# Three buffers for the first product's weights, and `w_out`'s groups loaded one by one

## The chip, the cores and the metric

The kernel runs on one core of a Trainium2 chip. The metric is the device time of one execution in microseconds (us); each kernel is told by the median of several runs.

## The reference, cut to what matters

```python
# attention: B, H, S, D = 4, 8, 768, 64
q_bits = (q @ proj > 0)                       # 6 bits per row, as one bucket number
k_bits = (k @ proj > 0)
scores = D**-0.5 * q @ k.T                    # where the buckets differ: -1e9
attn   = softmax(scores) @ v
# bridge: (B, H, S, D) -> x of 3072 x 512
h   = x @ w_in                                # 512 x 2048
g   = maximum(h, 0) + alpha * minimum(h, 0)
out = g @ w_out                               # 2048 x 512
```

All inputs and the output are float32 to the kernel's eye; the two weights arrive as pairs of words, which the kernel rounds and joins.

## The kernel before, in words

**Attention.** The function `fast_path` works on 16 pairs of heads (4 batches of 4), each in two units of 384 queries: 32 units of about 10 us. In a unit PE computes scores for 6 blocks of keys (L734), ACT takes their exponential into one of ten `pt` tiles (L739), and PE multiplies these by `v` (`attend`, L767). The sum over the keys is made of two halves: DVE adds blocks 0 and 1 into `accp` and GpSimd's queue (POOL) issues a transfer that adds block 2 to it on the way (`add_first`, L748 and L749); DVE adds blocks 3 to 5 into `accd` (L753, L754) and then `accp` to it (`add_total`, L757). PE sums `accd` over the partitions (`totals`, L779), DVE and GpSimd turn this into a divisor, and the result `x` is stored to device memory (`x_s`, L809).

**Weights.** Beside attention the 32 pieces of the two weights are loaded (`raw`, L567), rounded on ACT and DVE, and stored again. `w_in` goes, with the sums that the fast product below needs, to `w_in_s` (L648): 8 groups of 7 matrices. `w_out` goes as it is to `w_out_r` (L635), in 8 groups; its sums are made later.

**The MLP.** Both products use seven multiplications of half-size blocks in place of eight (the class `Product`). Per batch of 768 tokens there are 8 blocks of the first product, named f_0 to f_7, and 7 of the second, named z_1 z_2 z_5 z_6 z_3 z_7 z_4 in their order. A block's steps are groups of matmuls into PSUM banks `a`, `b`, `c`; ACT copies some of them out, DVE adds others and applies the activation (L896, L900, L904). PE is written to begin the next block (`now.step(1)`) before it makes the last step of the one before (`before.step(4)`), so that f_2a's first group stands ahead of f_1a's last.

- `load_w(n)`, L829, loads a block's seven matrices of `w_in_s` into a `wi` tile (896 KB, tag `wi`, two buffers). `load_w(0)` and `load_w(1)` are called in attention, at unit 18; block n's own pass calls `load_w` for n + 2, whose buffer is free when block n's last step is done.
- `load_out(n)`, L934, loads two groups of `w_out_r` into one `wo` tile (2 transfers of 512 KB on GpSimd's queue). The tile shares its tag `wl` and two buffers with the second product's weights.
- `sum_out(n)`, L942, makes a group's four sums on DVE (L946) and stores the group to `w_out_s` (L947, GpSimd's queue). The sums are spread by hand over the first seven blocks of batch 0 (0; 1; 2; 3 and 4; 5; 6 and 7, in blocks 1 to 6). Every second call loads two more groups.
- `load_w2(b, n)`, L923, loads the second product's weights (1 MB) into a `wl` tile, from `w_out_r` or `w_out_s`, on SP's queue; DVE makes further sums of it (`ws`, L964) and of `g` (`gs`, L972). In batch 0 the first two of these loads take over the buffers of the last `wo` tiles, and so wait for the stores of groups 4 to 7.
- In block 4 of batch 0 four small transposes on PE and some tiny DVE instructions check the inputs' magnitude (`verdict`); for inputs out of range a general path would run after it.

**What sets the order.** Instructions of PE, DVE, ACT and most of GpSimd are kept in the order of the program (`do` is `tc.keep_in_program_order`). Transfers on SP's queue and GpSimd's are not: the framework places each by its own planning, and gives it the waits that its buffers and data need. Tiles live in pools; the pool `sb` of attention is closed when attention ends, and the pool `late` opens over its memory. The pool `mid` (with `wi`) and `const` last for the whole program.

The line numbers here and below are those of the kernel before.

Of the kernel before, what the change touches and what calls it, by code (L numbers as in the profile page):

```python
# [8 lines left out]
F32 = mybir.dt.float32  # L9
BF16 = mybir.dt.bfloat16  # L10
# [396 lines left out]
def fast_path(  # L407
# [12 lines left out]
    nc = tc.nc  # L420
    P = 128
    B, H, S, D = q.shape
    NB = proj.shape[1]
    NTOK, DM = out.shape
# [20 lines left out]
    const = ctx.enter_context(tc.tile_pool(name="const", bufs=1))  # L445
    dram = ctx.enter_context(tc.tile_pool(name="dram", bufs=1, space=bass.MemoryType.DRAM))
    mid = ctx.enter_context(tc.tile_pool(name="mid", bufs=2))
    psum = ctx.enter_context(tc.tile_pool(name="ps", bufs=1, space=bass.MemoryType.PSUM))
    attn = ctx.enter_context(ExitStack())
    pool = attn.enter_context(tc.tile_pool(name="sb", bufs=2))  # L450
# [13 lines left out]
    alpha = const.tile([P, NF], F32, name="alpha")  # L464
    mags = const.tile([P, 2, NPAIR], F32, name="mags")

    qbs = [const.tile([P, S], BF16, name=f"qb{i}") for i in range(2)]
    NI = NF // 2
    NM = 7
    w_in_s = dram.tile([NI, P, NM, 2, P], F32, name="w_in_s")  # L470
    w_out_r = dram.tile([4, P, NI, DM // 2], F32, name="w_out_r")
# [31 lines left out]

    def setup():

        zero = const.tile([P, 512], BF16, name="zero")
        do(DVE.memset(zero, 0.0))
        do(DVE.memset(wh, 0.0))
        for s in range(2):
            nc.sync.dma_start(wh[D * s : D * s + D, :NB], proj)  # L510
        nc.sync.dma_start(alpha16, moe_alpha.rearrange("(t p) -> t p", p=P))
        make_identity(nc, ident)
        do(DVE.memset(ones, 1.0))

        ps = psum.tile([P, 512], F32, name="nil", tag="av")
        nil.append(lambda: do(PE.matmul(ps, zero[:, :P], zero, start=True, stop=True)))
        for i in range(7):
            nil[0]()

        do(DVE.memset(hb, 0.0))  # L520
        for r in range(0, P, 32):
            do(DVE.memset(hb[r : r + 2 * NB], 1.0 if r % D else -1.0))
            do(DVE.memset(hb[r : r + NB], -1e-37))

        do(DVE.tensor_scalar(hb_k[:, 0:1], hb, -1.0, None, op0=ALU.mult))
        do(DVE.memset(hb_k[:, 1:2], 0.0))
        for r in range(0, P, 32):
            do(DVE.memset(hb_k[r : r + 2 * NB, 1:2], 0.5))
        for t in pts:
            do(POOL.memset(t[:, :, CW : CW + 1], 1.0))  # L530
        for t in qbs:
            do(POOL.memset(t, 0.0))
# [9 lines left out]
    HW = NW // 2  # L542
# [39 lines left out]
    def weight_clamp(i):  # L582
        if i < NW:
            i = order[i]
            x = wx[i]
            do(DVE.tensor_scalar(x, x, HI_MIN, None, op0=ALU.max, op1=ALU.max, accum_out=wmax[:, i : i + 1]))
# [225 lines left out]
    x_m, w_m, g_m = {}, {}, {}  # L812

    def load_x(b):
        for m, kh, ch in ((0, 0, 0), (1, 1, 0), (2, 1, 1), (5, 0, 1)):
            t = mid.tile([P, 2, CW], F32, name=f"x{b}_{m}", tag=f"x{m}", bufs=1)
            nc.sync.dma_start(
                t, x_s[b, 2 * kh : 2 * kh + 2].rearrange("k p s -> p k s")[:, :, ch * CW : (ch + 1) * CW],
            )
            x_m[b, m] = t  # L820
# [8 lines left out]
    def load_w(n):  # L829

        if n < B * NI:
            w_m[n] = mid.tile([P, NM, 2, P], F32, name=f"wi{n}", tag="wi")
            nc.sync.dma_start(w_m[n], w_in_s[n % NI])

    class Product:
# [96 lines left out]
    w_o = {}  # L932

    def load_out(n):  # L934

        if n < NI:
            t = late[0].tile([P, 2, 4, DM // 2], F32, name=f"wo{n}", tag="wl")
            for i in range(2):
                nc.gpsimd.dma_start(t[:, i], w_out_r[:, :, n + i].rearrange("m p d -> p m d"))
                w_o[n + i] = t[:, i]  # L940

    def sum_out(n):  # L942

        w = w_o[n]
        for to, x, op, y in ((2, 3, ALU.add, 2), (3, 0, ALU.subtract, 3), (0, 2, ALU.subtract, 0), (1, 1, ALU.subtract, 0)):
            do(DVE.tensor_tensor(w[:, to], w[:, x], w[:, y], op=op))  # L946
        nc.gpsimd.dma_start(w_out_s[:, :, n].rearrange("m p d -> p m d"), w)  # L947
        if n % 2:
            load_out(n + 3)

    def sides_g(b, n):
        t = g_m[b, SIDES[ORDER[n]][1]]
# [100 lines left out]
    def verdict():  # L1053
        ps = psum.tile([1, 4, P], F32, name="vd", tag="sm")
        for n in range(4):
            do(PE.transpose(ps[:, n], top[:, n : n + 1], ident))
        do(DVE.tensor_reduce(row, ps, axis=mybir.AxisListType.X, op=ALU.max))
        do(DVE.tensor_tensor(row[:, 0:1], row[:, 0:1], row[:, 1:2], op=ALU.mult))

        do(DVE.tensor_scalar(row[:, 0:1], row[:, 0:1], SAFE, None, op0=ALU.is_le))  # L1060
        do(DVE.tensor_scalar(row[:, 2:3], row[:, 2:3], HI_END, None, op0=ALU.is_lt))
        do(DVE.tensor_scalar(row[:, 3:4], row[:, 3:4], 1.0, None, op0=ALU.is_le))
        do(DVE.tensor_tensor(row[:, 0:1], row[:, 0:1], row[:, 2:3], op=ALU.mult))
        do(DVE.tensor_tensor(row[:, 0:1], row[:, 0:1], row[:, 3:4], op=ALU.mult))
        do(DVE.tensor_scalar(flag, row[:, 0:1], -1.0, 1.0, op0=ALU.mult, op1=ALU.add))
# [37 lines left out]
    for u in range(UNITS):  # L1103
        pi, g = divmod(u, NCH)

        def weight_rest():
            weight_sum(u)
            weight_group(u)
            weight_clamp(u + 1)

        scores(u, 1)
        if u < last:
            scores(u + 1, 0)
        if u:
            divide(u - 1, weight_rest)
        else:
            weight_clamp(1)
        load_weight(u + 3)
        add_last(u)
        add_total(u)  # L1120
        if u < last:
            add_first(u + 1)
        else:
            now = ff1(0, 0)
            now.step(1)
            now.step(5)
        if g == 0 and pi + 1 < NPAIR:
            hash_bits(pi + 1)
        if g == 1 and pi + 2 < NPAIR:
            turn(pi + 2, "q")  # L1130
            turn(pi + 2, "k")
        if u < last:
            weight_parts(u + 1)
        weight_sums(1)
        attend(u)
        totals(u)
        if u == last:
            divide(u)
        if g == 1 and pi + 2 < NPAIR:
            load(pi + 2, "v")  # L1140
        if u == HW + 2:
            load_w(0)
            load_w(1)
            load_x(0)
        if HW + 4 <= u < HW + 8:
            sum_x(0, u - HW - 4, DVE)
        if u + 2 < NW:
            weight_abs(u + 2)
        if u == 1:
            setup_alpha()  # L1150
        if g == 1:
            for name in "qk":
                magnitude(pi, name)
                if pi + 3 < NPAIR:
                    load(pi + 3, name)


    late = []
    attn.close()
    late.append(ctx.enter_context(tc.tile_pool(name="late", bufs=2)))  # L1160
    load_out(0)
    load_out(2)
    blocks = [(b, what, n) for b in range(B) for what, count in (("1", NI), ("2", 7)) for n in range(count)]


    for j, (b, what, n) in enumerate(blocks):
        n2 = n + 1 if what == "2" else 0 if n == NI - 1 else 7
        if n2 == 0:
            sides_g(b, 0)
            sum_w2(b, 0, 3, 4)  # L1170
        now.step(2) if j else now.step(6)
        if j == 0:
            now.step(3)
            now.step(7)
            now.step(2)
        now.step(22)
        if j == 4:
            largest()
        if 0 < n2 < 7:
            sides_g(b, n2)  # L1180
            sum_w2(b, n2, 3, 4)
        if n2 < 7:
            sum_g2(b, n2, 3, 4)
        if j:
            now.step(5)
            now.step(6)
            now.step(3)
            sum_w2(b, n2, 6)
            now.step(7)
            sum_w2(b, n2, 5)  # L1190
            sum_g2(b, n2, 5)
        if j == 4:
            verdict()
        for n_out in [(), (0,), (1,), (2,), (3, 4), (5,), (6, 7)][j] if j < 7 else ():
            sum_out(n_out)
        if what == "1":
            load_w(b * NI + n + 2)

            if 0 <= n - NI + (4 if b else 2) < 2:
                load_w2(b, n - NI + (4 if b else 2))  # L1200
        else:
            load_w2(b, n + 2)
            if b + 1 < B:
                if n == 0:
                    load_x(b + 1)
                if n == 6:
                    for m in range(4):
                        sum_x(b + 1, m, DVE)
        if j + 1 < len(blocks):
            turn_out()  # L1210
        else:
            turn_last(0)
        before = now
        if j + 1 < len(blocks):
            b1, what1, n1 = blocks[j + 1]
            now = ff1(b1, n1) if what1 == "1" else ff2(b1, n1)
            now.step(1)
        before.step(4)
        if n2 < 7:
            sum_g2(b, n2, 6)  # L1220
# [29 lines left out]
```

## Time and profile before

| | |
|---|---|
| median of 7 runs | 905.38 us (903.31 to 906.36) |
| the profiled execution: its own time, its span | 903.01 us, 901.2 us |
| busy: PE, PEld, DVE, ACT, POOL | 887.6, 591.0, 754.8, 408.8, 100.4 us |
| granted PE clock | 1.00 |
| moved by DMA | 146.88 MB, mean 163 GB/s |
| `wi` loads | 32 of 896 KB, 4.6 us to landing (median) |
| `wo` loads and stores | 8 and 8 of 512 KB, 5.8 and 4.8 us (median) |
| `accp` transfers | 32 of 384 KB, 5.2 us (median) |

PE is TensorE's matmuls, PEld its weight loads, DVE is VectorE, ACT ScalarE, POOL GpSimd, SP SyncE, whose queue (SPq) issues most transfers. In a timeline a row has its start and length in us from the span's start, the engine, the line, the operation with out<-in and shapes, the number of instructions merged, and in brackets the idle time before it with what ended it. The lines themselves stand in the prediction. Attention lasts until about 350 us in this execution; the four batches of the MLP follow, 136 us each.

### The profile page before, as it was taken

The numbers are of one execution on the slowest core, as the hardware profiler recorded it, in microseconds if no ns is written. First come the engines' busy times: TensorE is split into PE (matmuls) and PEld (weight loads), VectorE is DVE, ScalarE is ACT, GpSimd is POOL, SyncE is SP. The second block draws the span as 40 slices with busy tenths as digits, with TensorE's granted clock in tenths as the row PEclk, the third lists the DMA queues.
The fourth block names the chain that finished last, engine by engine and source line by source line (L and its number), as shares of the span: only waits on it lengthen the run. The fifth ranks groups of instructions, "written<-read, shape, count | busy, mean of one in ns | idle before, by whom it ended". The sixth has DMA issues, their size and how long they took to land.

```text
span 901.2 us, 15654 instructions
## 1 busy us (share of the span) xinstructions
PE 887.6 (98%) x5885; PEld 591.0 (66%) x5885; DVE 754.8 (84%) x1353; ACT 408.8 (45%) x733; POOL 100.4 (11%) x194
## 2 busy tenths in 40 slices
PE   8999999999999999999999999999999999999996
PEld 4444445444444445556997557998557998556996
DVE  4888988988998996799989668988768989768985
ACT  6888888887888863222112222112222111222111
POOL 1222222222222232120000000000000000000000
PEclk9999999999999999999999999999999999999999
DMA  8778889698798665478343525243525242521242
GB/s 222 177 200 181 204 224 219 167 268 236 166 245 204 179 160 189 155 239 301 135 154 86 183 85 190 94 158 82 187 83 192 95 158 75 194 83 41 95 147 67
DMA packets 131909, 146.88 MB, mean 163 GB/s; under 512 B 78304, under 2 KB 118000, under 8 KB 128240
## 3 DMA queue, kind: packets, MB, share of 16 engines
q1 hardware_dynamic: 118800, 124.03, 44.4%
q0 software_dynamic: 11008, 20.97, 11.8%
q8 instruction: 48, 0.79, 0.4%
q10 hardware_dynamic: 2016, 0.79, 0.3%
q14 instruction: 37, 0.30, 0.1%
HBM read 104.87 MB, written 28.31 MB: 148 GB/s over the span
## 4 chain that ended last, share of the span: by engine, by line
PE 93%; DMA 3%; DVE 1%; SPq 0%; issue 0%; ACT 0%; ACTq 0%
PE sc L734 17%; PE av L767 14%; PE z_2a L854 2%; PE f_0a L854 2%; PE f_2a L854 2%; PE f_5a L854 2%; PE z_4a L854 2%; PE z_7a L854 2%; PE z_3a L854 2%; PE z_6a L854 2%; PE z_5a L854 2%; PE f_3a L854 2%; PE f_6a L854 2%; PE f_4a L854 2%; PE f_1a L854 2%; PE z_1a L854 2%
## 5 line engine op out<-in xcount | busy, mean ns | idle before, releaser
L739 ACT ACTIVATE pt<-sc 128x768 f32<-128x768 f32 x192 | 152.8, 813 | 46.6 <-PE sc L734 44.3
L734 PE MATMUL sc<-qT,kT 64*128 64x384 f32 x768 | 155.3, 482 | 0.0
L767 PE MATMUL av<-pt,vn 128*32 128x384 f32 (+1 forms) x1536 | 130.6, 488 | 0.0
L767 PEld LDWEIGHTS av<-pt,vn 128*32 128x32 f32 x1536 | 46.6, 109 | 75.1 <-issue 72.9
L734 PEld LDWEIGHTS sc<-qT,kT 64*128 64x128 f32 x768 | 68.2, 188 | 35.1 <-issue 34.9
L904 DVE TENSOR_TENSOR g<-g,g 128x384 f32<-128x384 f32 x128 | 68.4, 555 | 2.2
L734 PE MATMUL sc<-qb,kb 64*128 64x384 bf16 x384 | 63.4, 324 | 2.1 <-ACT kb L722 1.0
L749 POOL DMA_DIRECT2D accp<-pt x32 | 38.6, 1205 | 191.2 <-issue 86.5
L972 DVE TENSOR_TENSOR gs<-g,gs 128x768 f32<-128x768 f32 x56 | 53.3, 952 | 1.0
L964 DVE TENSOR_TENSOR ws<-wl 128x512 f32<-128x512 f32 x56 | 38.5, 687 | 17.8 <-DMA wl<-w_out_s 15.9
L972 DVE TENSOR_TENSOR gs<-g 128x768 f32<-128x768 f32 x56 | 53.3, 951 | 0.0
L900 DVE SCALAR_TENSOR_TENSOR g<-h,alpha 128x384 f32<-128x384 f32 x32 | 19.7, 617 | 26.8 <-ACT h L893 26.8
L734 PEld LDWEIGHTS <-kb 64*128 64x128 bf16 x384 | 19.3, 94 | 33.4 <-issue 11.3
L711 ACT ACTIVATE qb<-hs,hb 32x384 bf16<-32x384 f32 x62 | 35.5, 572 | 1.1
L757 DVE TENSOR_TENSOR accd<-accd,accp 128x768 f32<-128x768 f32 x32 | 30.7, 958 | 4.4 <-DMA accp<-pt 3.4
L754 DVE TENSOR_TENSOR accd<-accd,pt 128x768 f32<-128x768 f32 x32 | 30.7, 958 | 3.3
L748 DVE TENSOR_TENSOR accp<-pt,pt 128x768 f32<-128x768 f32 x32 | 30.5, 952 | 2.7 <-ACT pt L739 2.7
L753 DVE TENSOR_TENSOR accd<-pt,pt 128x768 f32<-128x768 f32 x32 | 30.4, 949 | 0.0
L803 POOL COPY rr<-rr 32x6 f32<-32x6 f32 x64 | 27.6, 431 | 2.6
L984 DVE TENSOR_TENSOR m<-m,m 128x768 f32<-128x768 f32 (+1 forms) x36 | 27.1, 751 | 0.7
L722 ACT ACTIVATE kb<-hs,hb 64x384 bf16<-64x384 f32 (+1 forms) x47 | 27.1, 577 | 0.6
L802 POOL COPY rr<-rr 32x6 f32<-32x6 f32 x64 | 19.8, 310 | 65.5 <-DVE rr L799 64.2
(336 smaller groups left out, 1807.2 us busy)
## 6 DMA issues: line engine op xcount, KB each, us to landing
wi<-w_in_s SPq DMA_DIRECT2D x32, 896.0 KB, 4.6
wl<-w_out_s SPq DMA_DIRECT2D x16, 1024.0 KB, 4.8
accp<-pt POOLq DMA_DIRECT2D x32, 384.0 KB, 5.2
wl<-w_out_r SPq DMA_DIRECT2D x12, 1024.0 KB, 4.8
raw<-in_moe_w_out_dram SPq DMA_DIRECT2D x16, 512.0 KB, 5.3
raw<-in_moe_w_in_dram SPq DMA_DIRECT2D x16, 512.0 KB, 4.6
w_in_s<-wsi SPq DMA_DIRECT2D x16, 448.0 KB, 5.8
vn<-in_v_dram SPq DMA_DIRECT2D x16, 384.0 KB, 6.1
```

The costliest lines, as they stand in the source:

```text
L711: do(ACT.activation(bits["q", pi][D * s : D * s + 32, cols], ps["q"][c : c + 32, half, :CW], AF.Sign, bias=hb[c : c + 32],))
L734: do(PE.matmul(sc[:, s, :CW], what["k", pi][r, ks], what["q", pi][r, qs], start=first, stop=not first,))
L739: do(ACT.activation(pt[:, :, :CW], sc[:, :, :CW], AF.Exp, scale=SCALE / DOWN))
L748: do(DVE.tensor_tensor(accp[u], p(u, 0), p(u, 1), op=ALU.add))
L749: nc.gpsimd.dma_start(accp[u], p(u, 2), accum_op=ALU.add)
L754: do(DVE.tensor_tensor(accd[u], accd[u], p(u, 5), op=ALU.add))
L757: do(DVE.tensor_tensor(accd[u], accd[u], accp[u], op=ALU.add))
L767: do(PE.matmul(av[u][D * s + t : D * s + t + 32, :w], nat["v", pi][:, s, kc * D + t : kc * D + t + 32], prob[u, kc][:, s, :w], start=(kc = ...
L854: do(PE.matmul(self.ps[bank], self.left(left, k), self.right(right, k), start=start and k == 0, stop=k == self.nk - 1, skip_group_check=no ...
L904: do(DVE.tensor_tensor(new_g(b, to)[:, i], g_m[b, x][:, i], g_m[b, y][:, i], op=ALU.subtract))
L964: do(DVE.tensor_tensor(t, w2[b, n, x], w2[b, n, y], op=op))
L972: do(DVE.tensor_tensor(t, g2[b, n, x], g2[b, n, y], op=ALU.subtract))
```

## The change

The first product's weights get three buffers. Their third load is called in attention, at unit 25, and every block then calls the load for three blocks ahead. To make room, the tiles `qb` and `zero`, which only attention uses, go from the lasting pool to attention's own. `load_out` loads one group instead of two; group 0 is loaded as before ahead of the blocks, and the others are called in blocks 0 to 4 (1; 2; 3; 4 and 5; 6 and 7), instead of groups 1 to 3 with it and the rest behind sums 1 and 3.

```diff
-    qbs = [const.tile([P, S], BF16, name=f"qb{i}") for i in range(2)]
+    qbs = [pool.tile([P, S], BF16, name=f"qb{i}", bufs=1) for i in range(2)]
...
-        zero = const.tile([P, 512], BF16, name="zero")
+        zero = pool.tile([P, 512], BF16, name="zero", bufs=1)
...
-            w_m[n] = mid.tile([P, NM, 2, P], F32, name=f"wi{n}", tag="wi")
+            w_m[n] = mid.tile([P, NM, 2, P], F32, name=f"wi{n}", tag="wi", bufs=3)
             nc.sync.dma_start(w_m[n], w_in_s[n % NI])
...
     def load_out(n):
 
-        if n < NI:
-            t = late[0].tile([P, 2, 4, DM // 2], F32, name=f"wo{n}", tag="wl")
-            for i in range(2):
-                nc.gpsimd.dma_start(t[:, i], w_out_r[:, :, n + i].rearrange("m p d -> p m d"))
-                w_o[n + i] = t[:, i]
+        if n % 2 == 0:
+            w_o[n] = late[0].tile([P, 2, 4, DM // 2], F32, name=f"wo{n}", tag="wl")
+        nc.gpsimd.dma_start(w_o[n - n % 2][:, n % 2], w_out_r[:, :, n].rearrange("m p d -> p m d"))
 
     def sum_out(n):
 
-        w = w_o[n]
+        w = w_o[n - n % 2][:, n % 2]
         for to, x, op, y in ((2, 3, ALU.add, 2), (3, 0, ALU.subtract, 3), (0, 2, ALU.subtract, 0), (1, 1, ALU.subtract, 0)):
             do(DVE.tensor_tensor(w[:, to], w[:, x], w[:, y], op=op))
         nc.gpsimd.dma_start(w_out_s[:, :, n].rearrange("m p d -> p m d"), w)
-        if n % 2:
-            load_out(n + 3)
...
             load_x(0)
+        if u == HW + 9:
+            load_w(2)
...
     load_out(0)
-    load_out(2)
...
         for n_out in [(), (0,), (1,), (2,), (3, 4), (5,), (6, 7)][j] if j < 7 else ():
             sum_out(n_out)
+        for n_out in [(1,), (2,), (3,), (4, 5), (6, 7)][j] if j < 5 else ():
+            load_out(n_out)
         if what == "1":
-            load_w(b * NI + n + 2)
+            load_w(b * NI + n + 3)
```

## The prediction

> **What bounds the kernel now.** I read the chain of waits first: PE holds 93% of it, DMA 3%, so a gain is a gap on PE that closes. Then the list of what PE's matmuls waited for, over the whole span (waiter, line, releaser: us in total, times, longest):
> ```profile
> PE f_7a L854 <- DMA wi<-w_in_s: 1.0, 1, 1.0
> PE f_2a L854 <- DMA wi<-w_in_s: 0.9, 1, 0.9
> PE z_2a L854 <- DMA wl<-w_out_r: 0.4, 1, 0.4
> ...
> PE f_5a L854 <- DMA wi<-w_in_s: 0.2, 1, 0.2
> ```
> Only four waits lie in the MLP, all in batch 0, where the `wi` loads share the DMA engines with the `wo` loads and stores. What each costs is read from the timeline of the weight loads, since these normally run ahead of their matmuls. Around f_2a:
> ```profile
> 358.91 1.16 PEld L854 LDWEIGHTS f_1a<-x,wi 128*128 128x128 f32 x4
> 361.57 0.94 PEld L854 LDWEIGHTS f_2a<-x,wi 128*128 128x128 f32 x4 [1.50 <-DMA wi<-w_in_s]
> 362.64 1.16 PEld L854 LDWEIGHTS f_1a<-x,wi 128*128 128x128 f32 x4
> ```
> Undisturbed groups of four follow each other every 1.29 us. Two groups took 362.64 - 358.91 = 3.73, so f_2a lost 3.73 - 2.58 = 1.15 us. The same reading gives f_7a 1.24 (406.16 to 409.98) and z_2a 0.69 (425.67 to 428.96, groups of 1.30). f_5a gives 0.95 (387.15 to 390.68), but the verdict's four transposes stand in that place and take about 0.5, which leaves 0.45. In all 3.5 us are lost.
>
> Next, VectorE and the other engines at the end of the first product:
> ```profile
> 408.54 0.56 DVE L896 TENSOR_TENSOR f_6p<-f_6p,f_6u 128x384 f32<-128x384 f32 x1 [0.21 <-ACT f_6u L861]
> 408.90 1.56 PE L854 MATMUL f_7a<-x,wi 128*128 128x384 f32 x4 [0.97 <-DMA wi<-w_in_s]
> 409.67 3.51 DVE L946 TENSOR_TENSOR wo<-wo 128x256 f32<-128x256 f32 x8
> ...
> 413.48 0.75 POOL L947 DMA_DIRECT2D w_out_s<-wo  x1 [0.44 <-DVE wo L946]
> ...
> 422.79 0.33 SPq L928 DMA_DIRECT2D wl<-w_out_r  x1
> ...
> 427.71 1.58 PE L854 MATMUL z_2a<-g,wl 128*128 128x192 f32 x8 [0.42 <-DMA wl<-w_out_r]
> ...
> 428.16 0.69 DVE L964 TENSOR_TENSOR ws<-wl 128x512 f32<-128x512 f32 x1
> ...
> 431.35 0.35 DVE L990 TENSOR_TENSOR m<-z_1u,z_1c 128x192 f32<-128x192 f32 x1
> ```
> and the busy time by window (PE, PEld, DVE, ACT, POOL, clock, DMA share, GB/s):
> ```profile
> 399.00:408.50 9.50, 8.94 (x28) 4.94 (x26) 9.01 (x18) 2.86 (x6) 2.25 (x3) 1.00 0.76 259
> 408.50:418.00 9.50, 9.10 (x28) 5.43 (x29) 9.08 (x19) 1.92 (x5) 1.52 (x2) 1.00 0.68 230
> 418.00:428.00 10.00, 9.58 (x55) 8.73 (x54) 9.82 (x17) 2.23 (x6) 0.00 (x0) 1.00 0.95 361
> ```
> See that DVE has no room here: apart from 0.21 us before f_6p it works through from 389.5 to 428, because the sums of `wo` (L946, 8 x 0.43 = 3.5 us in block 6) stand in its order. PE's gaps before f_5a and f_7a lie beside this backlog. And z_2a waits for a load that SP could issue only at 422.79, when the store of the last sum (issued 413.48) had landed 9.2 us later, at a DMA share of 0.95.
>
> Last, the place in attention where the new early load goes:
> ```profile
> 191.45 1.28 SPq L648 DMA_DIRECT2D w_in_s<-wsi  x2
> 192.78 3.21 SPq L833 DMA_DIRECT2D wi<-w_in_s  x2
> 196.09 1.16 SPq L567 DMA_DIRECT2D raw<-in_moe_w_out_dram  x1
> ...
> 202.23 1.20 POOL L749 DMA_DIRECT2D accp<-pt  x1 [6.53 <-ACT qn L686]
> ...
> 211.26 0.96 DVE L757 TENSOR_TENSOR accd<-accd,accp 128x768 f32<-128x768 f32 x1 [1.62 <-DMA accp<-pt]
> ...
> 213.03 0.13 PEld L779 LDWEIGHTS sm<-accd,ones 128*32 128x32 f32 x4 [0.19 <-issue]
> ```
> The windows there show a DMA share of 0.97 to 1.19 from 185 to 220. An accumulating transfer that lands in 5.2 us (median) took 8.9, DVE waited 1.62 us for it, and PE's use of the sum came only 0.8 us after DVE's add (211.26 + 0.96 = 212.22 against 213.03).
>
> **What the Trainium skill says.** "DMA: Bandwidth & Descriptors", section "Issuing engines are not separate DMA queues": transfers of SP and POOL run on the same 16 engines and interleave. The trace agrees: a `wi` load takes 4.5 us with little beside it (the one issued at the end of f_2) and 7.3 behind the four `wo` loads (issued 354.26). The same page, "Queues, rings and completion order", has each engine go round the queues packet by packet, so a POOL transfer would hardly feel a deeper SP queue. The trace looks more like order of arrival (those 7.3 us); I use both as bounds below. "TensorE: Matmul & The Clock Gate", section "Step-by-step: what each phase is for": weight loads are pulled ahead of running matmuls. The trace agrees: undisturbed loads begin 0.32 us before their matmuls, at f_2a both begin at 361.57, and so a late buffer costs about 0.3 us more than the matmul row's idle time.
>
> **The change part by part.** Sums are made against the profiled execution: 903.01 us, its span 901.2. The median of the seven runs is 905.38, 2.4 us above; I subtract the gain from the median.
>
> (1) `qb` and `zero` move to a pool that closes with attention; `wi` gets a third 7 KB buffer. No instruction and no transfer is added: 32 loads of 896 KB before and after. The pool that opens there starts with the `wo` loads, which wait for all engines already (350.19); the first sum reads at 362.42 what landed at 353.9 (3.7 us after its issue), so 8.5 us cover any delay; beyond that it would cost what the first sum is late. Cost nothing.
>
> (2) Every `wi` load from the fourth on is issued one block (9 us) ahead of before. In the compiled SP queue wi3 stands exactly where wi2 stood, wi4 where wi3 stood, and so on; the first batch's traffic at every point is the same in bytes. A load of 7.3 us with some 17 us to go instead of 8 is never late. f_2a gains its whole 1.15 us: DVE still has idle time there (6.87 of 9 us busy from 361 to 370), so nothing else holds PE.
>
> f_5a's 0.45 and f_7a's 1.24 disappear where they are, but what counts is what PE meets next. DVE's order is unchanged and full from 389.5 on; it gains only its 0.21 us wait at f_6p. The sums of groups 6 and 7, their stores and the load behind them come from that DVE chain, hence wl for z_2a lands at most about 0.2 us sooner, in the same saturated DMA. PE arrives earlier by 1.24 + 0.45 and waits at z_2a instead of at f_7a. Were wl early, z_2c still waits for DVE's L990 at 431.35 (0.16 us of wait already now), and that chain can gain 0.21 + 0.18 (its gap before 428.16). So f_5a, f_7a and z_2a together give between 0 and 0.4; I take 0.2. One later gap of 0.05 (f_2a of the last batch) goes too. MLP: 1.15 + 0.2 + 0.05 = 1.4.
>
> (3) The load of wi2 goes to attention. It is written at unit 25, but nothing holds it there: the compiled SP queue has it right behind wi1, ahead of the raw weight load of 196.09. It waits for the store issued at 191.45, which landed 8.1 us later, 199.6. So SP stands from 196.0 to 199.6, then issues for 0.3 to 2.0 us. Behind it queue a raw weight (read by ACT at 213.78, landed at 207.4), an x store, q, v and k of later pairs (first needed by PE at 218.75; landed by 214): all have 4 us or more in hand. What has not is the accumulating transfer of POOL. wi2 adds 0.92 MB, 2.3 us at the 406 GB/s of that stretch. Below: 0 us later, if queues are served in turn or if q's loads (ahead of it before) now fall behind it. A gain is excluded, since PE has no gap there to close. Above: all 2.3 us, of which PE pays 2.3 - 0.8 = 1.5. I take 0.9 us later, 0.1 paid by PE, because the held loads, about 1.3 us of work, drop behind the transfer and offset more than half of wi2.
>
> (4) The `wo` loads one by one: the POOL queue of the compiled program has the same 8 loads and 8 stores in the same order with the same waits. Loads 0 to 3 wait for nothing but the pool, so they still leave at once from 350.19; loads 4 to 7 still wait for the stores that free their buffer (379.81, 399.11). Nothing moves, in either direction; DVE's, ACT's and PE's orders are unchanged too.
>
> Sum: 1.4 - 0.1 = 1.3 us; 905.4 - 1.3 = 904.1 us.
>
> **The rivals.** A, the above: 904.1, its own range 903.8 to 904.8 (1.15 + 0.4 + 0.05 = 1.6 at best with nothing paid; 1.2 won and 0.6 paid in attention at worst).
>
> B, all three `wi` stalls are won and z_2a's does not grow: PE's 1.15 + 0.45 + 1.24 = 2.8, giving 902.6; with z_2a's 0.69 on top 901.9. For it: DVE's waits could be shorter than they look, since its rows overlap by a few hundredths. Against it: 9.82 of 10 us busy, and the store chain of 413.48.
>
> C, attention loses more than the MLP gains. The place is the matmul of the totals at 213.03, the price one us per us by which the accumulating transfer is late beyond 0.8. It decides from 0.8 + 1.4 = 2.2 us late on. If the held loads interleave with it as well (their own work 1.3 us and q's, about 0.8), it is 2.3 + 1.3 + 0.8 = 4.4 late and PE pays 3.6: 905.4 - 1.4 + 3.6 = 907.6. For it: 1.62 us of waiting there already and a DMA share above 1. Against: these loads were ahead of it before too.
>
> D, the change does not do what it says: the spread is none in any case (part 4); if wi2's stall were taken over by a wait of f_3a or by DVE at once, the time stays 905.4. Against it: DVE's idle time from 361 to 389.
>
> **How the numbers follow.** A 0.58, B 0.20, C 0.12, D 0.10. About 0.2%, 1.8 us, is what a measurement of this kernel can tell from no change. Below 903.6 lie B's 0.20 and what scatter of the medians may take A there, 0.06: faster 0.26. C's heavier two thirds and a little of the unforeseen, 0.10, are slower by more. The rest, 0.64, is within. For eight in ten: down to 902.3 takes in all but B's far end, up to 906.3 leaves out most of C.
>
> **What would show it.** Right: no wait of f_2a, f_5a, f_7a for wi; a longer wait of z_2a for wl (about 1.5 to 2 us instead of 0.4); `wo` loads still together at about 349; DVE solid from 388 to 427; an SP gap of about 4 us at 196; PE's totals near 213 late by at most half a us. Wrong: z_2a waits no longer than before (B), or PE waits for the sums at 213 or in the unit after it by over 2 us (C), or new waits of f_3a.

## The result and the profile after

| | before | after |
|---|---|---|
| median | 904.69 us (903.05 to 907.75, 36 runs) | 902.08 us (900.62 to 904.29, 15 runs) |
| ratio | | 0.9972, 95% interval 0.9963 to 0.9981: 1.7 to 3.3 us faster |
| the profiled execution: its own time, its span | 903.01, 901.2 us | 900.33, 898.5 us |

The gain of 2.6 us is twice the predicted 1.3, and 902.08 lies below the 902.3 to which the range reached. The line numbers of the changed kernel are 1 to 4 lower from `load_out` on (the sums of `wo` are L944, DVE's adds into `m` L986).

First PE's waits for transfers in the changed kernel. Of the four of before one is left:
```profile
PE z_2a L854 <- DMA wl<-w_out_r: 1.7, 1, 1.7
```
The weight loads around f_2a now follow each other every 1.29 us, without a gap:
```profile
358.27 1.16 PEld L854 LDWEIGHTS f_1a<-x,wi 128*128 128x128 f32 x4
359.56 1.16 PEld L854 LDWEIGHTS f_2a<-x,wi 128*128 128x128 f32 x4
360.85 1.16 PEld L854 LDWEIGHTS f_1a<-x,wi 128*128 128x128 f32 x4
```
The load behind f_2a stood at 362.64 and stands at 360.85, 1.79 sooner; the one ahead of f_2a stood at 358.91 and stands at 358.27, 0.64 sooner. So f_2a won 1.15 us against this profile of before, as predicted. The load that SP issues at that place took no less time to land (8.5 us, 7.3 before), but it is now the one of a later block. The end of the first product, all engines:
```profile
406.45 0.55 DVE L896 TENSOR_TENSOR f_6p<-f_6p,f_6u 128x384 f32<-128x384 f32 x1
...
407.57 3.52 DVE L944 TENSOR_TENSOR wo<-wo 128x256 f32<-128x256 f32 x8
...
411.38 0.75 POOL L945 DMA_DIRECT2D w_out_s<-wo  x1 [0.44 <-DVE wo L944]
...
421.14 0.33 SPq L928 DMA_DIRECT2D wl<-w_out_r  x1
...
425.92 1.57 PE L854 MATMUL z_2a<-g,wl 128*128 128x192 f32 x8 [1.71 <-DMA wl<-w_out_r]
```
See the chain that did not get shorter: last sum, store issued at 411.38, load behind it only at 421.14 (9.8 us; 9.3 before), z_2a at 425.92. (These are long landings: the eight stores of `wo` in the profile of before have a median of 6.6 us, not the 4.8 of the table of before, and its eight loads 5.5, not 5.8.) PE came there early, and gave back what f_5a and f_7a had won.

A way to compare executions: count the matmuls, and take the time between the same two of them. From a matmul of f_1 (at 356) to one of z_5 (at 433 to 442 in the profiles of this study), which holds all stalls of batch 0, before took 81.22 us and after 79.94: 1.28 less, which is the predicted 1.3. The other 1.4 us by which these two profiles differ (their spans: 2.7) lie at the start, where the changed kernel is 0.6 ahead within 19 us, and behind the last matmul, where its end comes 0.7 sooner. Nothing in the change was meant to act there. So the first question was whether these belong to it all the same, and whether the two profiles are typical: the profiled execution of the changed kernel, at 900.33 us, was faster than all 15 runs behind its median.

### The profile page after: what moved, and what is told of

The parts are those of the page before. It is cut to its first block, busy times and chain, and to the rows that moved or that the text cites. A ratio compares the mean times of both kernels' runs of the same rounds, so it can differ in the third digit from the quotient of the medians.

```text
span 898.5 us, 15656 instructions
## 1 busy us (share of the span) xinstructions
PE 886.3 (99%) x5885; PEld 591.0 (66%) x5885; DVE 754.2 (84%) x1353; ACT 408.7 (45%) x733; POOL 100.4 (11%) x194
## 4 chain that ended last, share of the span: by engine, by line
PE 92%; issue 3%; DMA 3%; ACT 1%; POOL 1%; DVE 0%; ACTq 0%; POOLq 0%; SPq 0%
PE sc L734 17%; PE av L767 14%; PE z_2a L854 2%; PE f_0a L854 2%; PE z_4a L854 2%; PE z_7a L854 2%; PE z_3a L854 2%; PE z_6a L854 2%; PE z_5a L854 2%; PE f_1a L854 2%; PE f_2a L854 2%; DMA w_out_s<-wo 2%; PE z_1a L854 2%; PE f_7a L854 2%; PE f_6a L854 2%
```

## The experiments

Four kernels first: each half of the change by itself, the memory moves by themselves, and the change again. The ratios are all against runs of before on the same chip.

**wi_alone**: the third buffer, with the moves of `qb` and `zero`, and the early third load; `load_out` and its calls as before.

> The third wi buffer, the memory moves it needs and the early third load, with the loads of w_out as they were before. The theory (the wi stalls alone make the gain, the loads of w_out nothing): ratio 0.997, the same 2.5 us as the whole change; in the profile f_2a, f_5a and f_7a without a wait, z_2a waiting about 1.7 us, last matmul 1.9 us earlier than before. The rival (part of the gain comes from the loads one by one): only the 1.3 us that the MLP showed, ratio 0.9986.

Measured: 902.65 us against 904.21, ratio 0.9984 (0.9977 to 0.9990). That is the rival's number, but not for the rival's reason: the whole change, run again on the same chip (**after_again** below), gives no more, so the loads one by one add nothing. z_2a waited 2.1 us, but the last matmul came 0.5 us later than in the profile of before, not 1.9 earlier: a miss that the part on the clock below explains for the most part.

**moves_alone**:
```diff
-    qbs = [const.tile([P, S], BF16, name=f"qb{i}") for i in range(2)]
+    qbs = [pool.tile([P, S], BF16, name=f"qb{i}", bufs=1) for i in range(2)]
...
-        zero = const.tile([P, 512], BF16, name="zero")
+        zero = pool.tile([P, 512], BF16, name="zero", bufs=1)
```


> Only qb and zero move to the pool that closes with attention; wi stays at two buffers, loads as before. The theory (memory addresses don't matter): ratio 1.000, within 0.5 us, and the 0.6 us by which the first product of the changed kernel came sooner is not there, or comes and goes by chance. The rival (where these tiles lie changes the start): ratio 0.9993, 0.6 us, with the first matmuls 0.6 us earlier than before.

Measured: 904.29 against 904.21, ratio 1.0004 (0.9994 to 1.0015). The moves cost and give nothing that this can tell (the interval reaches from 0.5 us faster to 1.4 slower). Over the twelve profiles of this study the same early matmul starts anywhere from 16.14 to 17.15 us, and from the end of the last matmul to the end of the span pass 6.8 to 8.3 us: start and tail vary without regard to the edits.

**out_alone**: the diff's `load_out`, `sum_out` and calls of `load_out`, nothing else.

> Only w_out's groups loaded one by one, two wi buffers, tiles where they were. The theory (the queue of POOL holds the same transfers in the same order with the same waits): ratio 1.000, within 0.5 us, wo loads together at about 349, f_2a waiting 0.9 us for wi as before. The rival (the spread is real): wo loads 1 to 3 some 9 us apart, f_2a's wait gone, ratio 0.9985.

Measured: 904.42 against 904.21, ratio 0.9998 (0.9986 to 1.0009). The four `wo` loads leave together, as before:
```profile
349.76 3.06 POOL L938 DMA_DIRECT2D wo<-w_out_r  x4 [2.00 <-issue]
```

**after_again**: the changed kernel once more.

> The whole change once more, for the size of the scatter between profiles: the theory expects a ratio of 0.9972 to 0.9986, the MLP's shift of 1.3 us the same to 0.1 us, and the shifts of 0.6 us at the start and 0.8 us behind the last matmul to change by some tenths of a us, being chance. The rival (they belong to the change): both again within 0.15 us.

Measured: 902.65 against 904.21, ratio 0.9983 (0.9975 to 0.9990), 1.6 us; the stretch from f_1 to z_5 took 80.26, so its shift is 0.96 and not 1.28, more apart than expected. The end behind the last matmul took 8.2 us this time, 6.8 in the first profile. Both measurements of the changed kernel together (36 runs) have a median of 902.48; the kernel before has 904.21 to 904.70 beside the kernels of this study. That is about 2.0 us.

What was not chance showed in the two kernels with two `wi` buffers: their f_2a stalls were more than twice as long as in the profile of before. Weight loads of moves_alone:
```profile
358.10 1.16 PEld L854 LDWEIGHTS f_1a<-x,wi 128*128 128x128 f32 x4
361.95 0.62 PEld L854 LDWEIGHTS f_2a<-x,wi 128*128 128x128 f32 x3 [2.69 <-DMA wi<-w_in_s]
...
366.00 1.16 PEld L854 LDWEIGHTS f_2b<-x,wi 128*128 128x128 f32 x4 [0.25 <-issue]
```
Three groups took 7.90 us instead of 3.87: 4.0 lost, where the profile of before lost 1.15. Were these edits to blame, or was that profile a lucky one? So the kernel before was run again, together with three that act on the two stalls.

**before_again**: no edit.

> The kernel before once more, for the size of its stalls. The theory (its first profile fell on a small stall): f_2a waits between 0.9 and 2.6 us for wi, likelier near the upper end, and its time is 903 to 906 us. The rival (the larger stalls of the two kernels with two buffers come from their edits): f_2a waits 0.9 us to within 0.2.

Measured: 904.56 us. PE's waits in its profile:
```profile
PE f_2a L854 <- DMA wi<-w_in_s: 1.8, 1, 1.8
...
PE f_5a L854 <- DMA wi<-w_in_s: 1.1, 1, 1.1
...
PE f_7a L854 <- DMA wi<-w_in_s: 1.0, 1, 1.0
...
PE z_2a L854 <- DMA wl<-w_out_r: 0.3, 1, 0.3
```
The same kernel waits twice as long for the same load. So the edits need not be to blame, and the first profile had fallen on a short stall.

**spread_two**: two `wi` buffers, loads one by one as in out_alone, and in `load_out` ahead of the transfer:
```diff
+        if 0 < n < 4:
+            do(DVE.memset(w_o[n - n % 2][:, n % 2, 0, 0:1], 0.0))
```


> Two wi buffers; w_out's groups loaded one by one and really held back: a write of one column by VectorE, in its program order, stands ahead of the loads of groups 1 to 3. The theory (f_2a's stall is the wi load queued behind four w_out loads): the wi load issued at about 354 lands in 5 us instead of 7.3 to 9.0, f_2a doesn't wait, about 2.5 us won there; z_2a's wait stays or grows; ratio 0.998. The rival (the late issue alone makes the stall): f_2a still waits 0.9 us or more, ratio 1.000.

Measured: 902.69 against 904.44, ratio 0.9981 (0.9973 to 0.9988). Loads on POOL and PE's weight loads:
```profile
349.81 0.80 POOL L940 DMA_DIRECT2D wo<-w_out_r  x1 [2.00 <-issue]
...
353.18 0.76 POOL L940 DMA_DIRECT2D wo<-w_out_r  x1 [2.57 <-DVE wo L939]
...
359.82 1.16 PEld L854 LDWEIGHTS f_2a<-x,wi 128*128 128x128 f32 x4
...
364.87 0.75 POOL L940 DMA_DIRECT2D wo<-w_out_r  x1
```
The `wo` loads now do leave one by one, and f_2a doesn't wait, though its load was issued at 353.88, as late as ever (354.26 before): with two `wo` loads ahead of it instead of four it landed after 5.6 us. So the stall came from the `wo` loads ahead of it. A spread that really takes place is worth as much as the third buffer (1.8 us against 1.6).

**sums_early**: the kernel wi_alone, and
```diff
-        for n_out in [(), (0,), (1,), (2,), (3, 4), (5,), (6, 7)][j] if j < 7 else ():
+        for n_out in [(0,), (1,), (2,), (3, 4), (5,), (6, 7), ()][j] if j < 7 else ():
```


> Three wi buffers as in the change; the sums of w_out's groups each one block earlier (the last two in the sixth block instead of the seventh), so that the second load of the second product's weights no longer waits for their stores. The theory (with the wi stalls gone what is left of the gain is held at z_2a by this load, 1.7 to 2.1 us of waiting in three profiles): no wait of z_2a, ratio 0.996, 1.5 to 2.5 us faster than the changed kernel. The rival (VectorE's full chain holds TensorE there in any case): z_2c waits for VectorE instead, ratio 0.998, no faster than the changed kernel.

Measured: 899.61 against 904.44, ratio 0.9946 (0.9934 to 0.9957): 4.8 us faster than before, more than expected, and the fastest kernel of the study (six runs, 898.52 to 900.56). In its timeline:
```profile
402.46 0.75 POOL L947 DMA_DIRECT2D w_out_s<-wo  x1 [0.44 <-DVE wo L946]
...
409.27 0.32 SPq L928 DMA_DIRECT2D wl<-w_out_r  x1
...
423.66 1.33 PEld L854 LDWEIGHTS z_2a<-g,wl 128*128 128x128 f32 x8
```
Against the changed kernel the last store leaves 9 us sooner, the load behind it 12 us sooner, and z_2a's weights are loaded without a wait. PE waits for no transfer in the MLP any more. The rival falls: z_2c doesn't wait for VectorE either, since the sums themselves have gone out of its full stretch.

**sums_early_two**: the same edit to the kernel before, with two buffers.

> The same earlier sums with the kernel before's two wi buffers. The theory (the stall of z_2a and those of wi are separate losses): f_2a waits for wi as before, 0.9 to 2.6 us, z_2a does not wait, ratio 0.9985. The rival (the earlier sums and stores only push traffic onto the wi loads): new or longer waits of f_3a to f_6a, ratio 1.000 or above.

Measured: 904.33 against 904.44, ratio 0.9994 (0.9981 to 1.0007). The rival is right here. The longest of PE's waits:
```profile
PE f_7a L854 <- DMA wi<-w_in_s: 2.2, 1, 2.2
PE f_6a L854 <- DMA wi<-w_in_s: 1.3, 1, 1.3
PE f_4a L854 <- DMA wi<-w_in_s: 1.2, 1, 1.2
```
z_2a waits no more, but PE now waits for the late `wi` loads; that the earlier stores and loads of `wo` delay them is the likely reason, not one shown apart. The profile is of the slowest execution (908.95) of fourteen that range from 901.68, so these waits are long ones. By the medians the same edit is worth some 3 us on top of the third buffer (4.8 less 1.6) and nothing without it.

A last pair asked for the spread on top of the buffers, and for the price of the early load in attention.

**spread_three**: the changed kernel with the `memset` of spread_two.

> The changed kernel with the loads of w_out's groups 1 to 3 really held back by a one-column write of VectorE, as in the run with two buffers. The theory (the third buffer covers a late landing already, and z_2a's wait comes from the last sums): f_2a doesn't wait, z_2a waits about 2 us as in the changed kernel, ratio 0.998, within 0.7 us of the changed kernel. The rival (the spread adds to the buffers' gain): ratio 0.9965.

Measured: 902.52 against 904.70, ratio 0.9980 (0.9972 to 0.9987); z_2a waited 2.1 us. As the theory has it: with three buffers the spread has nothing left to win that this measurement can tell.

**wi2_own**: every third `wi` tile comes from the pool that opens after attention.
```diff
-            w_m[n] = mid.tile([P, NM, 2, P], F32, name=f"wi{n}", tag="wi", bufs=3)
+            own = n % 3 == 2
+            w_m[n] = (late[0] if own else mid).tile([P, NM, 2, P], F32, name=f"wi{n}", tag="wi2" if own else "wi", bufs=1 if own else 2)
...
-        if u == HW + 9:
-            load_w(2)
...
+    load_w(2)
     load_out(0)
```


> The changed kernel with the third wi buffer in the pool that opens after attention, so that the third wi load leaves at about 350 instead of 196; all else as in the changed kernel. The theory (the early load costs attention nothing, and a load at 350 is still in time for f_2a): attention as long as in the changed kernel to 0.1 us, no gap on SP's queue at 196, f_2a without a wait, ratio 0.998. The rival (the early load in attention costs 0.5 us or more, or the load at 350 delays the first w_out sums): ratio 0.9973, or 0.999.

Measured: 901.85 against 904.70, ratio 0.9971 (0.9962 to 0.9979). SP's queue in attention, first in the changed kernel:
```profile
192.11 7.09 SPq L833 DMA_DIRECT2D wi<-w_in_s  x3
199.30 0.38 SPq L567 DMA_DIRECT2D raw<-in_moe_w_out_dram  x1
```
then in wi2_own:
```profile
192.89 4.46 SPq L834 DMA_DIRECT2D wi<-w_in_s  x2
197.44 0.91 SPq L567 DMA_DIRECT2D raw<-in_moe_w_out_dram  x1
```
The early load holds SP's queue until 199.3, as predicted, and in the changed kernel VectorE's wait for `accp` near 211 grows from 1.62 to 2.55 us, by the 0.9 that was predicted. Yet from a matmul at 225 to one at 356 us pass 130.80 us in the changed kernel and in wi2_own, 130.81 in before, and from 157 to 225 us 67.84 or 67.85 in all three. Attention paid nothing there. The ratio is nevertheless the rival's (0.9973), not the expected 0.998. It is 0.7 us better than spread_three's on the same chip, but the two intervals overlap, and no profile shows where such a gain would lie. (In spread_three's profile the stretch from 225 took 0.8 us more, with two waits of PE for VectorE's `x`; after, after_again, wi_alone and sums_early, which have the early load too, took 130.80. Whether the early load costs something in some executions stays open.)

**The stalls of batch 0, in one table.** Time lost against sums_early, which has no stall there: from f_1 to a matmul of f_2 (11.61 us in sums_early), and from there to z_5 (66.28 us).

| kernel | f_2a | f_5a, f_7a, z_2a | PE clock fell |
|---|---|---|---|
| before, first profile | 1.15 | 2.17 | |
| before_again | 2.07 | 2.98 | |
| out_alone | 2.89 | 3.05 | |
| moves_alone | 4.03 | 3.00 | at f_2a |
| after, first profile | 0 | 2.05 | |
| after_again | 0 | 2.37 | |
| wi_alone | 0 | 4.15 | at z_2a |
| spread_three | 0 | 4.09 | at z_2a |
| wi2_own | 0 | 1.87 | |
| spread_two | 0 | 2.76 | |
| sums_early_two | 1.29 | 6.87 | at f_7a |

The first four rows have two `wi` buffers and unhindered `wo` loads, and the same transfers in the MLP; they lose 2.5 us at f_2a on average (2.1 without what the fall of the clock cost in moves_alone, see below) and 2.8 behind it. The three rows of after, after_again and wi_alone, whose instructions and transfers have one order, lose 0 and 2.9 (2.3 without the fall).

**The clock.** In moves_alone PE's granted clock fell after the wait (windows: PE, PEld, DVE, ACT and POOL busy, clock, DMA share, GB/s):
```profile
360.00:362.00 2.00, 0.05 (x1) 0.05 (x1) 1.48 (x3) 0.45 (x1) 0.00 (x0) 1.00 0.04 16
362.00:364.00 2.00, 2.00 (x4) 1.11 (x5) 1.30 (x4) 0.00 (x0) 0.30 (x1) 0.63 0.00 0
364.00:366.00 2.00, 2.00 (x4) 1.01 (x3) 0.00 (x0) 0.48 (x1) 0.46 (x1) 0.52 0.50 176
```
and in wi_alone after z_2a's:
```profile
428.00:432.00 4.00, 4.00 (x16) 4.00 (x16) 3.97 (x7) 0.63 (x2) 0.00 (x0) 0.60 0.45 117
```
The price: the two groups from f_2a's start took 4.05 us in moves_alone (361.95 to 366.00) and 2.36 in before_again (361.88 to 364.24), 1.7 more. This is most of why wi_alone's profile missed its expectation. Five rests of PE of 2.07 us or more are in the MLP of the twelve profiles; four were followed by the fall (2.07, 2.07, 2.12, 2.17), one of 2.62 (out_alone) was not, and neither was any shorter one (the longest 2.03). Windows cut to the fall show half the clock for 3.4 us in each of the four, so that 1.7 us of work are lost. The Trainium skill, "TensorE: Matmul & The Clock Gate", section "What's actually happening", says that the clock is halved after an idle window of about 3.4 us, and that the window runs freely. The length of the falls agrees, and so does it that chance decides; the length of the rest does not, since half the clock came after 2.1 us.

How often this happens can be told roughly from each execution's mean clock. It is 0.995 or 0.996 in the four profiles with a fall and 0.997 or more in the eight others. In the five kernels with three buffers and the sums in their old place it is 0.996 or less in 27 of 102 runs, and these have medians 1.3 to 2.4 us above the rest; in the kernel before, in 18 of 131. (The mean also counts the clock behind the last matmul, so single runs can be sorted wrongly.) So PE's longer single wait at z_2a probably costs the changed kernel a fall in about every fourth execution.

## Why the prediction was wrong

- **The step that failed** is "f_2a gains its whole 1.15 us", and with it the sum "905.4 - 1.3 = 904.1 us". The mechanism was right: the stall is gone. The size was read from one execution, and this stall differs from one execution to the next: 1.15, 2.07, 2.89, 4.03 in four profiles with the same transfers, 2.5 on average, or 2.1 without the fall of the clock. With 2.5 or 2.1 in place of 1.15 the prediction's sum is 2.7 or 2.3 instead of 1.3. The first measurement has 2.6, the second 1.6, both together about 2.0. Four profiles are few, so the average itself is rough.
- The profile of before held a warning. The prediction noted that the profiled execution was 2.4 us faster than the median, and then took its gain off the median, as if the stalls of the two were the same. before_again, a slower execution (904.56 against 903.01), had 0.9 us more of stall at f_2a alone and 1.7 in batch 0. One such pair suggests the link, and does not prove it.
- The range's low end was built on that size too. Besides, the median of seven runs (905.38) stood 0.7 above that of 36 (904.69); of the 2.0 us between 904.1 and 902.08, 0.7 is this and 1.3 the gain.
- f_5a, f_7a and z_2a "together give between 0 and 0.4": right as far as these profiles can tell. z_2a's wait grew to 1.7 us (predicted 1.5 to 2), because the load behind the last store came hardly sooner after the last sum; the part behind f_2a loses 2.8 us on average with two buffers and 2.9 with three, or 2.3 without the fall of the clock in wi_alone. sums_early shows where it was held: let the last sums, and with them their stores and that load, go one block earlier, and 3 us more are won.
- That DVE's chain would hold PE near z_2c even with `wl` early was left open by the prediction and is not borne out where the sums move (sums_early). With the sums in their old place and only `wl` early it was not tried.
- Rival B came nearest in number (902.6), by luck, and was wrong in mechanism: it had z_2a's wait not grow. C, with attention losing more than the MLP gains, fell: the time went down, and attention took the same time between its matmuls. D fell: the time changed, though its remark that the spread does nothing is right.
- Part 4, that the loads one by one change nothing, is shown by out_alone; part 1, the memory moves, by moves_alone; part 3, attention, by the equal times between its matmuls (nothing paid where 0.1 was predicted).

What stays open: whether the gain is nearer 1.6 or 2.6 us (the two intervals overlap between 1.7 and 2.3), and why the same transfers land 7.3 us after the issue in one execution and 9.0 in another.

## What to carry to other kernels

A stall behind contended transfers is a distribution, not a number: before pricing it from one profile, take a second one, and ask how the profiled execution's time stands to the median; if it is faster, its stalls may be short ones. Calling a load later in the program does not move it when a framework places transfers: only something that it must wait for does, here a one-column write. A stall removed ahead of a store-to-load chain comes back at the end of that chain until its first link moves; look for the second edit that pays only beside the first.

## What the runs showed of the hardware

- PE's clock fell to half for 3.4 us after four of five rests of 2.07 to 2.62 us in the MLP, at 1.7 us each; after rests of 2.03 us and less, in these twelve profiles, it never did.
- When a load is issued can matter less than what was issued ahead of it: the same 896 KB load, issued at 353.5 to 354.3 behind four loads of 512 KB, let PE start after 7.3 us in one profile of before, 8.2 in the next, 8.5 and 9.0 in the two others with two buffers; behind two such loads (spread_two) it landed after 5.6 us.
